# Fewer and larger load transfers in a one-token decoder block, with V6's products placed among head 7's scores

## The chip, the cores and the metric

The kernel runs on one core of a Trainium2 chip. The metric is device time in microseconds (us), the median of several executions. A profile is one execution of its own, with its own time. Its span runs from the first to the last instruction and is a little shorter than that time.

## What is computed

One token passes through a block with adaptive layer norm: attention over a cache, then a feed-forward layer with ReLU. Sizes: D = 512, 32 query heads on 8 heads of K and V ("head" below means one of these 8), 32,768 cached keys of 128 elements, Dff = 1792, all in bfloat16.

```python
mod = (silu(c) @ w_mod).reshape(6, 512)      # sa, ca, ga, sb, cb, gb
h = layernorm(x) * (1 + ca) + sa
q = h @ wq                                   # 32 heads of 128
p = softmax(q @ k.T / sqrt(128))             # 4 query heads for each K head
x = x + ga * ((p @ v) @ wo)
h = layernorm(x) * (1 + cb) + sb
out = x + gb * (relu(h @ w1) @ w2)
```

K and V are 8.4 MB a head each, 134 MB in all; the weights are another 15 MB.

## The kernel before

All loads are issued on SyncE's queue (SP) by `stream_dma` (L154), in the order of the list `stream` (L162 to L169). They go into a ring of three slots of 64 KB a partition (`ring`, L81). A slot holds one whole K or V of a head, or w_mod and wq together, or the "tail": wo, w1 and w2. The slots are used in turn, so V6 follows K6, V7 follows V5, and the tail follows K7. A load is issued when the last reader of its slot's old content is done, and loads are issued strictly in order. A load's key is (kind, head, steps): a head has four steps of 64 keys a partition (`NTILE`), and a load covers all four, two, or one of them. Before the change, K6, K7, V5 and V6 come in halves (`halves`, from `HALVED` = 5 on), the order at the end is K7 first half, V6 first half, K7 second half, V6 second half, and then V7 as a half and two quarters. wo comes in four pieces (`WOP`, L47: heads 0 to 3, 4 and 5, 6, 7), w2 in five (`W2P`). The second half of K0 is split unevenly over three transfers (`UNEVEN`, L57 and L137). After V0's issue SP runs `SPACE` drains (L146).

The order of TensorE (PE) and VectorE (DVE) is written out by hand from L637 on. For each head h:

- `turn_k` (L429) transposes K in place on VectorE, in blocks of 32 x 32. Heads before the last are turned a step at a time (128x4096 of f32), the last head half a step at a time (128x2048).
- `scores` (L450) makes 8 products for each half step on TensorE (L460). Steps 0 and 1 fill the first PSUM bank of the tile `S_ps`, steps 2 and 3 the second.
- For the last head, `bank_max` (L465) takes the maximum of each bank on its own. `softmax` (L468) is a generator; each `next(soft)` emits one more stage: the maximum, its transpose to a row (L478), the row's maximum, its way back (L492), the exponential on ScalarE (L497), the transpose of P (L502), the sum (L506), its reciprocal (L509).
- `pv` (L515) multiplies P with V: 16 products for each step (L523). Heads up to 4 run it as a loop on the chip, later heads as single instructions; `js` selects some of a step's 16 products.
- `blocks` (L548) scales and sums the result on VectorE, `o_cols` (L559) puts it into a column, and `normalise` (L568) prepares it for wo when the last head of a wo piece is done. `spread` (L582) and `project` (L593) multiply with wo: the first two pieces (`WOROWS`) as rows, 16 and 8 products of 512 columns, the last two as columns, 16 small products each (L605). `join_rows` (L614) transposes the rows on VectorE (L617) and adds them to the columns (L622).
- `keep_clock` (L630) makes products that nobody reads.

Heads 1 to 6 run through the loop at L647, where the scores of head g + 1 stand ahead of the products of head g with V. Head 7 is written out behind it (L675 to L735): the first half of K7 is turned and scored, then come `blocks` of head 5, the maximum of the first bank, and the 32 products of the first half of V6 (L691). Then the second half of K7 is turned and scored, half a step at a time, and the softmax of head 7 follows, with the rest of V6's products between its stages. Behind these stand V7's products, the projection with wo, the second layer norm, w1 (L765) and w2 (L788).

Of the kernel before, what the change touches and what calls it, by code (L numbers as in the profile page):

```python
# [10 lines left out]
F32 = mybir.dt.float32  # L11
# [6 lines left out]
def kernel(  # L18
# [14 lines left out]
    nc = tc.nc  # L33
# [10 lines left out]
    NTILE = Sk // (P * TK)  # L44
    NG = NTILE // 2

    WOP = [(0, Hkv // 2), (Hkv // 2, Hkv // 4), (Hkv - 2, 1), (Hkv - 1, 1)]  # L47
    WOROWS = 2
    LAST = Hkv - 1
    LOOPED = Hkv - 2  # L50
    HALVED = LOOPED - 1
    W2P = [(0, 5), (5, 10), (10, 12), (12, 13), (13, 14)]
    W1P = [(0, KT)]

    OUT0, OUT1 = 30, 34

    UNEVEN, EDGE, MOST = ("k", 0, (2, 3)), 2 * TK * Dh - D // 2, 111  # L57
    SPACE = 14
    assert Dh == 128 and REP == 4 and D == 512 and FT == W2P[-1][1] and NTILE == 4
    scale = float(Dh) ** -0.5  # L60
    eps = 1e-5
# [50 lines left out]
    def load(key):  # L112
        kind = key[0]
        if kind == "wm":
            t = piece("wmq_sb", 0, WM).rearrange("p (kt n) -> p kt n", kt=KT)
            src = wm_v
        elif kind == "wq":
            t = piece("wmq_sb", WM, WQ).rearrange("p (kt n) -> p kt n", kt=KT)
            src = wq_v
        elif kind in "kv":  # L120
            g, steps = key[1], key[2]
            src = (kv if kind == "k" else vv)[g, :, TK * steps[0]:TK * (steps[-1] + 1), :]
            name = f"Ksb{g}" if kind == "k" else f"Vsb{g}"
            t = piece(name, TK * Dh * steps[0], TK * Dh * len(steps)).rearrange("p (j d) -> p j d", d=Dh)
        elif kind == "wo":
            g0, n = WOP[key[1]]
            t = piece("tail_sb", g0 * REP * D, n * REP * D).rearrange("p (r d) -> p r d", d=D)
            src = wo_v(key[1])
        elif kind == "w1":
            k0, k1 = W1P[key[1]]  # L130
            t = piece("tail_sb", WO + k0 * Dff, (k1 - k0) * Dff).rearrange("p (kt f) -> p kt f", f=Dff)
            src = w1_v[:, k0:k1]
        else:
            f0, f1 = W2P[key[1]]
            t = piece("tail_sb", WO + KT * Dff + f0 * D, (f1 - f0) * D).rearrange("p (f d) -> p f d", d=D)
            src = w2_v[:, f0:f1]
        if key == UNEVEN:  # L137
            row, src_row = (x.rearrange("p j d -> p (j d)") for x in (t, src))
            for rows, cols in (
                (slice(0, P), slice(0, EDGE)), (slice(0, MOST), slice(EDGE, None)), (slice(MOST, P), slice(EDGE, None)),  # L140
            ):
                stream_dma(row[rows, cols], src_row[rows, cols])
        else:
            stream_dma(t, src)
        if key[:2] == ("v", 0):
            for _ in range(SPACE):  # L146
                nc.sync.drain()
        if kind in "kv":
            for i, u in enumerate(steps):
                loaded[(kind, g, u)] = t[:, TK * i:TK * (i + 1), :]  # L150
        else:
            loaded[key] = t

    def stream_dma(dst, src):  # L154
        i = nc.sync.dma_start(out=dst, in_=src)  # L155
        tc.stamp_issue_order_token(i.ins, "sp_stream")
        if last_loop:

            tc.add_manual_dep(i.ins, last_loop[0], mybir.DependencyInfo(
                mybir.DependencyClass.NoSync, mybir.DependencyReason.DATA))  # L160
# [1 line left out]
    whole, halves = [(0, 1, 2, 3)], [(0, 1), (2, 3)]  # L162
    stream = [("k", 0, halves[0]), ("wm",), ("wq",), ("k", 0, halves[1])]
    for g in range(LOOPED):
        stream += [("k", g + 1, s) for s in (halves if g >= HALVED else whole)] + [("v", g, s) for s in (halves if g >= HALVED else whole)]
    for s in halves:
        stream += [("k", LAST, s), ("v", LOOPED, s)]
    stream += [("v", LAST, (0, 1)), ("v", LAST, (2,)), ("v", LAST, (3,))] + [("wo", i) for i in range(len(WOP))]
    stream += [("w1", i) for i in range(len(W1P))] + [("w2", i) for i in range(len(W2P))]  # L169
    pos = [0]  # L170
# [72 lines left out]
    pick8 = const.tile([16, 8], BF16)  # L243
    nc.vector.tensor_tensor(out=pick8[:], in0=ident_bf[0:16, 0:8], in1=ident_bf[0:16, 8:16], op=ALU.add)
    cx_sel = const.tile([16, 2], BF16)
    nc.vector.tensor_copy(out=cx_sel[:], in_=cmask[8][0:16, 0:2])
    cx_bd = piece("wmq_sb", R0 + 2048 + 4 * P, D)[0:16].rearrange("p (b n) -> p b n", b=8)
    nc.vector.tensor_tensor(  # L248
        out=cx_bd, in0=cx_row[:].unsqueeze(1).to_broadcast([16, 8, D // 8]),
# [179 lines left out]
    def turn_k(g, u, half):  # L429

        if u == 0 and half == 0:
            S_tiles[g] = two_banks("S_ps")
            m_tiles[g] = spool.tile([P, NG], F32, tag="m2", name="m2") if g == LAST else None
        Ksb = need(("k", g, u))
        KTt = Ksb[:, 32 * half:32 * half + 32, :].rearrange("p j d -> p (j d)")
        KT_tiles[g, u, half] = KTt
        if g == 0 and u < 2 or g < LAST and half:
            return
        if g < LAST:
            KTt = Ksb.rearrange("p j d -> p (j d)")  # L440
        t = nc.vector.transpose(out=KTt.bitcast(F32), in_=KTt.bitcast(F32))  # L441
        behind_loop(t)
# [7 lines left out]
    def scores(g, u, half):  # L450

        t4 = (2 * u + half) % 4
        if t4 == 0:
            S_ps_tiles[g] = S_tiles[g][:, u // 2, :]
        KTv = KT_tiles.pop((g, u, half)).rearrange("p (jj h i par) -> p jj h i par", jj=32, h=2, i=32, par=2)
        for sl in range(2):
            s = 2 * t4 + sl
            for hp in range(4):
                h, par = hp // 2, hp % 2
                nc.tensor.matmul(  # L460
                    S_ps_tiles[g], lhsT=qbd[g % 2][:, hp, 4 * (7 - s):4 * (7 - s) + P], rhs=KTv[:, 16 * sl:16 * sl + 16, h, :, par],
                    start=(t4 == 0 and sl == 0 and hp == 0), stop=(t4 == 3 and sl == 1 and hp == 3),
                )
# [101 lines left out]
    def part_of(g):  # L565
        return [i for i, (g0, n) in enumerate(WOP) if g0 <= g < g0 + n][0]
# [26 lines left out]
    def project(i):  # L593

        n = WOP[i][1] * REP
        wo_sb = need(("wo", i))
        for r in range(n):
            if i < WOROWS:
                nc.tensor.matmul(
                    a_rows[0][32 * (r % 4):32 * (r % 4) + 1, :], lhsT=o2_tiles[i][:, r:r + 1],  # L600
                    rhs=wo_sb[:, r, :], start=False, stop=(i == WOROWS - 1 and r >= n - 4), skip_group_check=True,
                )
                continue
            for ko in range(KT):
                nc.tensor.matmul(  # L605
                    attnT_ps[:, ko:ko + 1],
                    lhsT=wo_sb[:, r, :].rearrange("p (m ko) -> p ko m", ko=KT)[:, ko, :],
                    rhs=o2_tiles[i][:, r:r + 1], start=False, stop=(i == len(WOP) - 1 and r == n - 1),
                    skip_group_check=True,
                )  # L610

    a_rows = []

    def join_rows():  # L614

        aT = room("tail_sb", TAIL, [P, 512])
        nc.vector.transpose(  # L617
            out=aT.rearrange("p (a ko m) -> p a ko m", a=4, ko=KT),
            in_=a_rows[0].rearrange("p (a m ko) -> p a ko m", a=4, ko=KT),
        )  # L620
        for a in range(4):
            nc.tensor.matmul(  # L622
                attnT_ps[32 * a:32 * a + 32, :], lhsT=place32[:],
                rhs=aT.rearrange("p (a ko m) -> p a ko m", a=4, ko=KT)[:, a, :, 0],
                start=False, stop=False, skip_group_check=True,
            )

    spare = []
# [8 lines left out]
    with tc.manual_schedule(engines={mybir.EngineType.PE, mybir.EngineType.DVE}):  # L637
# [36 lines left out]
            next(soft)  # L674
        g, h = LOOPED, LAST  # L675
        build_qbd(h)
        turn_k(h, 0, 0)
        turn_k(h, 0, 1)
        next(soft, None)
        turn_k(h, 1, 0)  # L680
        turn_k(h, 1, 1)
        blocks(g - 1)
        scores(h, 0, 0)
        scores(h, 0, 1)
        scores(h, 1, 0)
        o_cols(g - 1)
        scores(h, 1, 1)
        normalise(g - 1)
        spread(part_of(g - 1))
        bank_max(h, 0)  # L690
        pv(g, (0, 1))  # L691
        for u in (2, 3):
            for half in range(2):
                turn_k(h, u, half)
                scores(h, u, half)
        bank_max(h, 1)
        soft = softmax(h)
        next(soft)
        next(soft)
        next(soft)  # L700
        pv(g, (2,), range(6))
        next(soft)
        next(soft)
        open_o(LAST)
        pv(g, (2,), range(6, 16))
        pv(g, (3,))
        next(soft)
        next(soft, None)
        end_b.append(two_banks("end_ps"))
        a_rows.append(row_bank(end_b[0][:, 0, :]))  # L710
        blocks(g)
        pv(LAST, (0, 1))
        o_cols(LAST - 1)
        normalise(LAST - 1)
        pv(LAST, (2,))
        spread(2)
        hid_ps = ps_o.tile([P, 512], F32, tag="o", name="hid_ps")
        nc.vector.memset(hid_ps[:], 0.0)
        pv(LAST, (3,))
# [3 lines left out]
        project(0)  # L723
        keep_clock(2)
        o_cols(LAST)
        keep_clock(2)
        project(1)
        normalise(LAST)
        spread(3)
        keep_clock(2)  # L730
        project(2)
        keep_clock(1)
        join_rows()
        keep_clock(1)
        project(3)  # L735


        stat2 = const.tile([P, 2], F32)
# [88 lines left out]
```

## Time and profile before

| | |
|---|---|
| median of 3 runs | 354.37 us (354.16 to 354.63) |
| the profiled execution's own time | 354.42 us |
| its span | 352.6 us |
| TensorE busy | 272.3 us (77%) |
| VectorE busy | 195.6 us (55%) |
| ScalarE busy | 18.7 us (5%) |
| bytes read from HBM | 149.42 MB, 424 GB/s over the span |
| granted TensorE clock, mean | 0.926 |

How to read it: the page of the profile gives the busy time of each engine, the span in 40 slices (a digit is the busy share in tenths), the queues of the DMA engines, and the chain of work that ended last, followed back from the last instruction to what released each step. The timeline lists instructions in order of time: start, length, engine, source line, operation, output and inputs with shapes, count, and in square brackets the idle time of the engine ahead of it with what ended that. The view by windows gives each engine's busy time in stretches of the span, with the granted clock of TensorE. PE is TensorE's products, PEld its weight loads, DVE VectorE, ACT ScalarE, POOL GpSimd, SPq the queue of SyncE.

### The profile page before, as it was taken

What the parts mean: (1) busy time and instruction counts of PE and PEld (TensorE: products, weight loads), DVE (VectorE), ACT (ScalarE), POOL (GpSimd) and SP (SyncE); (2) the same over time, 40 slices, a digit from 0 to 9 for tenths busy, and PEclk for the clock granted to TensorE, in tenths of its full rate; (3) what the DMA queues carried; (4) which work ended last, traced back from release to release, by engine and by line L of the source; (5) the groups of instructions that cost most, each with busy time, mean ns of one, the idle gap of its engine ahead of it and who ended that gap; (6) DMA issues with size and microseconds to landing.
All of it is one profiled execution on the core that took longest, in us unless ns stands there. A gap on an engine that the chain in (4) does not pass through costs nothing. (4 is left out here: it accounts for less than half of the span.)

```text
span 352.6 us, 3544 instructions
## 1 busy us (share of the span) xinstructions
PE 272.3 (77%) x1310; PEld 111.8 (32%) x1310; DVE 195.6 (55%) x167; ACT 18.7 (5%) x37; POOL 6.0 (2%) x26
## 2 busy tenths in 40 slices
PE   0054980695999679884988499976999999789994
PEld 0021330232333224331333233322444443234442
DVE  7662563983079513965099316956674293743142
ACT  1200003001000010001000100001000100011000
POOL 3000000000000000000000000000000000000000
PEclk9996895698999969998999979996999999999999
DMA  8999989999999999999999999999999999999995
GB/s 353 404 432 456 468 387 461 446 401 446 439 424 440 416 439 446 401 455 446 409 453 446 409 453 431 426 394 439 446 414 427 450 429 424 431 453 398 432 426 213
DMA packets 5222, 149.57 MB, mean 424 GB/s; under 512 B 604, under 2 KB 988, under 8 KB 1628
## 3 DMA queue, kind: packets, MB, share of 16 engines
q1 hardware_dynamic: 5180, 149.43, 98.5%
q8 instruction: 8, 0.13, 0.1%
q14 instruction: 2, 0.02, 0.0%
q10 hardware_dynamic: 32, 0.00, 0.0%
HBM read 149.42 MB, written 0.00 MB: 424 GB/s over the span
## 5 line engine op out<-in xcount | busy, mean ns | idle before, releaser
L441 DVE STREAM_TRANSPOSE Ksb<-Ksb 128x4096 f32<-128x4096 f32 (+1 forms) x34 | 131.5, 3912 | 57.6 <-DMA Ksb<-in_A_k_cache_dram 57.6
L460 PE MATMUL S_ps<-Ksb,qbd 128*128 128x512 bf16 x512 | 118.9, 385 | 19.2 <-DVE Ksb L441 18.3
L523 PE MATMUL o_ps<-Vsb,P_g 128*16 (+1 forms) x512 | 124.3, 401 | 10.9 <-ACT P_g L497 10.0
L460 PEld LDWEIGHTS <-qbd 128*128 128x128 bf16 x512 | 49.2, 97 | 84.9 <-issue 27.6
L523 PEld LDWEIGHTS o_ps<-Vsb,P_g 128*16 x320 | 30.4, 95 | 60.0 <-issue 31.8
L523 PEld LDWEIGHTS <-P_g 128*16 128x16 bf16 x192 | 16.7, 90 | 22.9 <-issue 0.4
L473 DVE TENSOR_REDUCE m_p<-S_ps 128x1 f32<-128x1024 f32 x7 | 8.6, 1223 | 21.8 <-PE S_ps L460 21.8
L502 DVE STREAM_TRANSPOSE P_g<-P_g 128x1024 bf16<-128x1024 bf16 x8 | 10.0, 1245 | 15.6 <-ACT P_g L497 15.6
L494 ACT ACTIVATE nbias<-Mb_ps 128x1 f32<-128x1 f32 x8 | 1.4, 171 | 269.5 <-PE Mb_ps L492 269.5
L324 PE MATMUL mod_ps<-wmq_sb,siluT 128*1 128x512 bf16 x24 | 3.6, 624 | 9.9 <-DMA wmq_sb<-in_w_mod_dram 9.9
L332 DVE STREAM_TRANSPOSE Ksb<-Ksb 128x4096 f32<-128x4096 f32 x2 | 8.8, 4424 | 1.7 <-DMA Ksb<-in_A_k_cache_dram 1.7
L478 PE MATMUL mT_ps<-ident_f,m_p 128*1 128x128 f32 x8 | 2.2, 270 | 8.9 <-DVE m_p L473 7.9
L497 ACT ACTIVATE P_g<-S_ps,nbias 128x1024 bf16<-128x1024 f32 x8 | 8.9, 1114 | 0.2
L560 PE MATMUL acc_ps<-mask_sb,Y 16*128 16x4 f32 x16 | 3.4, 282 | 5.1 <-DVE Y L556 5.1
L552 DVE SCALAR_TENSOR_TENSOR o_ps<-o_ps,Linv,smask 16x512 f32<-16x512 f32 x8 | 5.8, 720 | 2.8 <-PE o_ps L523 2.8
L254 PE MATMUL xc_ps<-cx_sel,wmq_sb 16*128 16x2 bf16 x4 | 0.3, 172 | 8.7 <-DVE wmq_sb L248 8.7
L590 DVE CAST o_sb<-o_ps 128x4 bf16<-128x4 f32 (+2 forms) x4 | 0.7, 167 | 11.1 <-PE o_ps L586 11.1
L415 POOL TENSOR_TENSOR qbd<-qrep_sb,rowpick 128x64 bf16<-128x64 bf16 x8 | 2.4, 299 | 228.0 <-PE S_ps L460 198.3
L509 DVE RECIPROCAL Linv<-L_ps 16x1 f32<-16x1 f32 x8 | 1.0, 126 | 8.3 <-PE L_ps L506 8.3
L556 DVE TENSOR_REDUCE Y<-o_ps 16x128 f32<-16x512 f32 x8 | 5.4, 679 | 0.3
L635 PE MATMUL spare_ps<-qbd,ident_bf 128*128 128x512 bf16 x18 | 5.4, 381 | 0.0
L396 PE MATMUL q_ps<-wmq_sb,hT 128*1 128x512 bf16 x32 | 3.6, 626 | 2.3 <-DMA wmq_sb<-in_A_wq_dram 2.3
(114 smaller groups left out, 71.6 us busy)
## 6 DMA issues: line engine op xcount, KB each, us to landing
Ksb<-in_A_k_cache_dram SPq DMA_DIRECT2D x5, 4096.0 KB, 22.9
Vsb<-in_A_v_cache_dram SPq DMA_DIRECT2D x5, 4096.0 KB, 36.5
wmq_sb<-in_A_wq_dram SPq DMA_DIRECT2D x1, 4096.0 KB, 28.1
Vsb<-in_A_v_cache_dram SPq DMA_DIRECT2D x2, 2048.0 KB, 41.1
Ksb<-in_A_k_cache_dram SPq DMA_DIRECT2D x1, 4032.0 KB, 37.2
wmq_sb<-in_w_mod_dram SPq DMA_DIRECT2D x1, 3072.0 KB, 18.9
tail_sb<-in_A_wo_dram SPq DMA_DIRECT2D x1, 2048.0 KB, 23.2
tail_sb<-in_B_w_dram SPq DMA_DIRECT2D x1, 1792.0 KB, 30.6
```

The lines of the kernel that those rows point to most:

```text
L324: nc.tensor.matmul(dst[j // 4][32 * (j % 4):32 * (j % 4) + 1, :], lhsT=src_T[:, kt:kt + 1], rhs=w[:, kt, j * 512:(j + 1) * 512], start=(kt ...
L332: nc.vector.transpose(out=t, in_=t)
L396: nc.tensor.matmul(q_ps[i][32 * a:32 * a + 1, :].rearrange("o (h e) -> o h e", e=32), lhsT=hT[:, kt:kt + 1], rhs=wq_f[:, kt, i, a], start= ...
L441: t = nc.vector.transpose(out=KTt.bitcast(F32), in_=KTt.bitcast(F32))
L460: nc.tensor.matmul(S_ps_tiles[g], lhsT=qbd[g % 2][:, hp, 4 * (7 - s):4 * (7 - s) + P], rhs=KTv[:, 16 * sl:16 * sl + 16, h, :, par], start= ...
L473: behind_loop(nc.vector.reduce_max(out=m_p[:], in_=S_g.rearrange("p g f -> p (g f)"), axis=AX.X))
L497: nc.scalar.activation(out=P_g[:], in_=S_g.rearrange("p g f -> p (g f)"), func=ACT.Exp, bias=nbias[:], scale=scale, accum_out=l_g[:],)
L502: behind_loop(nc.vector.transpose(out=P_g[:], in_=P_g[:]))
L523: nc.tensor.matmul(o_tiles[g][:], lhsT=PT, rhs=Vx, start=first, stop=False, skip_group_check=True)
L552: nc.vector.scalar_tensor_tensor(out=o, in0=o, scalar=Linv_tiles.pop(g)[:], in1=smask[:].unsqueeze(2).to_broadcast([16, 4, Dh]), op0=ALU.m ...
L556: nc.vector.tensor_reduce(out=Y[:], in_=o.rearrange("p s d -> p d s"), op=ALU.add, axis=AX.X)
L635: nc.tensor.matmul(spare[0], lhsT=ident_bf[:], rhs=qbd[0][:, :, 0:P], start=True, stop=True)
```

## The change

The list of loads has 29 entries in place of 37 transfers. K0's second half is one transfer again. K6, K7 and V5 come whole. The order at the end is K7, the two halves of V6, V7 as before, wo in two pieces (heads 0 to 3 and 4 to 7), w1, and w2 in four pieces. SP runs 19 drains in place of 14 after V0's issue.

In the part of head 7, `blocks` of head 5 comes first, then all eight half steps of K7 are turned, then all are scored. Behind each of the last four groups of scores stand three products of V6's step 0. `bank_max` of the first bank stands, on VectorE, behind the eight turns. The rest of V6's products follow in and behind the softmax of head 7: 4 of step 0, step 1, then steps 2 and 3 together.

At the end, both pieces of wo are used as rows with 16 products each, the second one only after head 7's result has been spread. The products as columns go. Six spare products stand ahead of the second piece and three behind it. The constant `cx_sel`, until now cut out of a mask for wo pieces of 8 rows, gets a small reduce of its own.

```diff
-    WOP = [(0, Hkv // 2), (Hkv // 2, Hkv // 4), (Hkv - 2, 1), (Hkv - 1, 1)]
-    WOROWS = 2
+    WOP = [(0, Hkv // 2), (Hkv // 2, Hkv // 2)]
-    W2P = [(0, 5), (5, 10), (10, 12), (12, 13), (13, 14)]
+    W2P = [(0, 6), (6, 11), (11, 13), (13, 14)]
-    UNEVEN, EDGE, MOST = ("k", 0, (2, 3)), 2 * TK * Dh - D // 2, 111
-    SPACE = 14
+    SPACE = 19
...
-        if key == UNEVEN:
-            row, src_row = (x.rearrange("p j d -> p (j d)") for x in (t, src))
-            for rows, cols in (
-                (slice(0, P), slice(0, EDGE)), (slice(0, MOST), slice(EDGE, None)), (slice(MOST, P), slice(EDGE, None)),
-            ):
-                stream_dma(row[rows, cols], src_row[rows, cols])
-        else:
-            stream_dma(t, src)
+        stream_dma(t, src)
...
     for g in range(LOOPED):
-        stream += [("k", g + 1, s) for s in (halves if g >= HALVED else whole)] + [("v", g, s) for s in (halves if g >= HALVED else whole)]
-    for s in halves:
-        stream += [("k", LAST, s), ("v", LOOPED, s)]
+        stream += [("k", g + 1, whole[0]), ("v", g, whole[0])]
+    stream += [("k", LAST, whole[0])] + [("v", LOOPED, s) for s in halves]
...
-    nc.vector.tensor_copy(out=cx_sel[:], in_=cmask[8][0:16, 0:2])
+    cx_half = const.tile([16, 2], F32)
+    nc.vector.tensor_reduce(
+        out=cx_half[:], in_=ident_f[0:16, 0:16].rearrange("p (c r) -> p c r", r=8), op=ALU.add, axis=AX.X,
+    )
+    nc.vector.tensor_copy(out=cx_sel[:], in_=cx_half[:])
...
         for r in range(n):
-            if i < WOROWS:
-                nc.tensor.matmul(
-                    a_rows[0][32 * (r % 4):32 * (r % 4) + 1, :], lhsT=o2_tiles[i][:, r:r + 1],
-                    rhs=wo_sb[:, r, :], start=False, stop=(i == WOROWS - 1 and r >= n - 4), skip_group_check=True,
-                )
-                continue
-            for ko in range(KT):
-                nc.tensor.matmul(
-                    attnT_ps[:, ko:ko + 1],
-                    lhsT=wo_sb[:, r, :].rearrange("p (m ko) -> p ko m", ko=KT)[:, ko, :],
-                    rhs=o2_tiles[i][:, r:r + 1], start=False, stop=(i == len(WOP) - 1 and r == n - 1),
-                    skip_group_check=True,
-                )
+            nc.tensor.matmul(
+                a_rows[0][32 * (r % 4):32 * (r % 4) + 1, :], lhsT=o2_tiles[i][:, r:r + 1],
+                rhs=wo_sb[:, r, :], start=False, stop=(i == len(WOP) - 1 and r >= n - 4), skip_group_check=True,
+            )
...
         build_qbd(h)
-        turn_k(h, 0, 0)
-        turn_k(h, 0, 1)
         next(soft, None)
-        turn_k(h, 1, 0)
-        turn_k(h, 1, 1)
         blocks(g - 1)
-        scores(h, 0, 0)
-        scores(h, 0, 1)
-        scores(h, 1, 0)
-        o_cols(g - 1)
-        scores(h, 1, 1)
-        normalise(g - 1)
-        spread(part_of(g - 1))
-        bank_max(h, 0)
-        pv(g, (0, 1))
-        for u in (2, 3):
+        for u in range(NTILE):
             for half in range(2):
                 turn_k(h, u, half)
+        for u in range(NTILE):
+            for half in range(2):
                 scores(h, u, half)
-        bank_max(h, 1)
+                if u >= 2:
+                    first = 3 * (2 * u + half - 4)
+                    pv(g, (0,), range(first, first + 3))
+                elif half:
+                    (o_cols if u == 0 else normalise)(g - 1)
+            if u % 2:
+                bank_max(h, u // 2)
         soft = softmax(h)
         next(soft)
         next(soft)
         next(soft)
-        pv(g, (2,), range(6))
+        pv(g, (0,), range(12, 16))
         next(soft)
         next(soft)
         open_o(LAST)
-        pv(g, (2,), range(6, 16))
-        pv(g, (3,))
+        pv(g, (1,))
         next(soft)
         next(soft, None)
         end_b.append(two_banks("end_ps"))
         a_rows.append(row_bank(end_b[0][:, 0, :]))
+        pv(g, (2, 3))
         blocks(g)
...
         pv(LAST, (2,))
-        spread(2)
...
         project(0)
         keep_clock(2)
         o_cols(LAST)
+        normalise(LAST)
         keep_clock(2)
+        spread(1)
+        keep_clock(6)
         project(1)
-        normalise(LAST)
-        spread(3)
-        keep_clock(2)
-        project(2)
-        keep_clock(1)
+        keep_clock(3)
         join_rows()
-        keep_clock(1)
-        project(3)
```

More of the change, by code (lines that the diff above doesn't have):

```diff
@@ L624, in join_rows @@
                 rhs=aT.rearrange("p (a ko m) -> p a ko m", a=4, ko=KT)[:, a, :, 0],
-                start=False, stop=False, skip_group_check=True,
+                start=False, stop=True, skip_group_check=True,
             )
```

## The prediction

> **What bounds the kernel now.** I read the page first: span, the load queue's share, the chain that ended last.
>
> ```profile
> span 352.6 us, 3544 instructions
> DMA  8999989999999999999999999999999999999995
> q1 hardware_dynamic: 5180, 149.43, 98.5%
> DMA 19%; PE 5%; DVE 3%; SPq 0%; issue 0%
> ```
>
> The queue of loads is busy for 98.5% of the span, and the chain is mostly DMA. The stream of loads sets the time; TensorE and VectorE have only to keep up and to free the three ring slots. Next, the same chain in order of time, for the last 80 us (start, length, what).
>
> ```profile
> 272.40 29.53 DMA Ksb<-in_A_k_cache_dram
> 301.96 8.90 DVE Ksb L441 x4
> 310.90 1.91 PE S_ps L460 x8
> 313.20 25.28 DMA tail_sb<-in_A_wo_dram
> 338.50 11.12 DMA tail_sb<-in_B_w_dram
> 349.66 0.29 PE end_ps L788 x4
> ```
>
> The second half of K7 lands at 301.93; four turns of it and its scores follow; they free the slot, and wo is issued into it at 313.2. The chain steps over to the queue there, but the queue isn't empty: wo lands 25 us later because V7 stands before it. The last w2 piece lands at 349.62, and 3.0 us of arithmetic end the span. What matters is how far the engines are behind those landings. The timeline of TensorE:
>
> ```profile
> 271.93 7.07 PE L523 MATMUL o_ps<-Vsb,P_g 128*16 128x512 bf16 x32
> 286.88 0.19 PE L506 MATMUL L_ps<-l_g,mask_sb 128*16 128x1 f32 x2
> 295.26 7.07 PE L523 MATMUL o_ps<-Vsb,P_g 128*16 128x512 bf16 x32
> 310.90 1.90 PE L460 MATMUL S_ps<-Ksb,qbd 128*128 128x512 bf16 x8 [0.30 <-DVE Ksb L441]
> 313.77 0.27 PE L478 MATMUL mT_ps<-ident_f,m_p 128*1 128x128 f32 x1 [0.97 <-DVE m_p L475]
> 313.98 1.46 PE L523 MATMUL o_ps<-Vsb,P_g 128*16 128x512 bf16 x6
> 315.52 5.78 PE L523 MATMUL o_ps<-Vsb,P_g 128*16 128x512 bf16 x26
> 321.39 7.07 PE L523 MATMUL o_ps<-Vsb,P_g 128*16 128x512 bf16 x32
> 332.36 3.62 PE L523 MATMUL o_ps<-Vsb,P_g 128*16 128x512 bf16 x16
> 336.08 1.03 PE L599 MATMUL end_ps<-tail_sb,o_sb 128*1 128x512 bf16 x16
> ```
>
> The first half of V6's products (295.26, 32 of them) is done while TensorE would else wait for K7's second half. After the last scores (312.80), 6 + 26 products of V6 and 64 of V7 remain, and V7's last ends at 335.98. Call that moment E. Behind it:
>
> ```profile
> 338.52 0.60 PE L599 MATMUL end_ps<-tail_sb,o_sb 128*1 128x512 bf16 x8
> 341.01 0.67 PE L605 MATMUL acc_ps<-o_sb,tail_sb 128*128 128x1 bf16 x16
> 341.71 0.16 DVE L740 TENSOR_TENSOR x1T<-acc_ps,modT_sb 128x4 f32<-128x4 f32 x1 [1.65 <-PE acc_ps L605]
> 345.33 0.93 PE L765 MATMUL hid_ps<-tail_sb,h2T 128*1 128x448 bf16 x16 [1.28 <-DMA tail_sb<-in_B_w_dram]
> 347.10 0.73 PE L788 MATMUL end_ps<-tail_sb 128*32 128x128 bf16 x20
> 349.98 0.28 DVE L793 TENSOR_TENSOR o_rows<-end_ps,gb_rows 34x128 f32<-34x128 f32 x1 [2.95 <-PE end_ps L788]
> ```
>
> W1's products wait 1.28 us for their load, so between E and the end the engines have about 2 us to spare, no more. A change that makes E later by over 2 us makes the kernel later.
>
> **The change, part by part.**
>
> *Fewer transfers.* Eight fewer. 1.5% of the span, 5.3 us, is all that the queue is not busy, its start and end included: 0.14 us for each of 37 transfers at the very most, 1.1 us for eight; at the least nothing. K0's second half loses its uneven split, at most 64 KB (0.15 us at 4,096 KB in 9.7 us, below) that move to other engines. I take nothing for the stream as a whole, being nearer to a queue without gaps, and keep -1.1 to +0.2 us for K7's landing.
>
> The Trainium skill's page "DMA: Bandwidth & Descriptors", section "Anatomy of one DMA", puts a fixed 2.0 us on each DMA (measured there for DMAs issued from GpSimd); eight fewer would by that estimate save 16 us. The 5.3 us that the queue lacks in all do not bear that out for transfers queued one behind another.
>
> *K7 ahead of all of V6.* At 272.40 three transfers of 4,096 KB stand in the queue (K7's first half, V6's first, K7's second) and take 29.53 us: about 9.7 us each after the rest of V5. Whole K7 therefore lands one transfer earlier than its second half did: 301.93 - 9.7 = 292.2. K6 lands whole five transfers before 301.93, at 253.5. Is VectorE free for K7?
>
> ```profile
> 258.09 8.74 DVE L441 STREAM_TRANSPOSE Ksb<-Ksb 128x4096 f32<-128x4096 f32 x2
> 232.38 3.64 PE L460 MATMUL S_ps<-Ksb,qbd 128*128 128x512 bf16 x16 [0.69 <-DVE Ksb L441]
> 292.36 0.68 DVE L556 TENSOR_REDUCE Y<-o_ps 16x128 f32<-16x512 f32 x1
> 295.45 0.68 DVE L466 TENSOR_REDUCE m<-S_ps 128x1 f32<-128x512 f32 x1
> ```
>
> K6's four turns (two in 8.74) end at 253.5 + 17.6 = 271.1, its last 16 scores at 274.8, against 272.0 before. V5's 64 products and the sums of head 6 follow as they do now (271.93 to 287.07, 15.1): 290.0. blocks(5), a product and a sum of about 0.7 each, ends at 291.5, before K7 is there. V6, K7's successor in the queue, is issued at 275 and V7 at 290, both with over 15 us of loads queued. The delay of 3 us is hidden by K7's own 19.4 us of transfer.
>
> *K7's turns and scores.* Here the change pays. VectorE now gets all eight turns in a row, then bank_max(7,0), the maximum over the first PSUM bank. Eight at 2.22 (8.90 for four): 292.2 + 17.8 = 310.0. TensorE does the scores of steps 0 and 1 behind the first four turns, until about 303. Then it should go on with step 2, turned at 303.3. In the program as built it can't: the first product of step 2 waits for a count of VectorE that only bank_max(7,0) brings (the turns of steps 2 and 3 no longer raise the count one by one), since it opens the second bank of the same tile that bank_max reads. Before, bank_max stood ahead of those turns (295.45), and the wait cost nothing. Now it stands behind all eight: 310.0 + 0.7 = 310.7. Queued behind the waiting product on TensorE is everything else: 3 products of V6 after each score group, the softmax, V6, V7, wo. So TensorE idles some 7.5 us with V6's first half landed (301.9) and unused.
>
> From 310.7, at 0.22 a product (7.07 for 32): 32 scores and the 9 products of V6 among them, 41 x 0.22 + 0.14 = 9.2: last score 319.9 (now 312.80). The maximum's way to the next transpose takes 0.97 as now: 320.9. Then 0.2, 4 products 0.9 and Mb: 322.05. V6's second step, 16 x 0.22 = 3.5, the sum 0.2, steps 2 and 3, 7.05: 332.8. V7's products with the column product between them now take 321.39 to 335.98, 14.6, of which 0.1 is a spread that goes: 14.5. E = 347.3, so far without a clock loss.
>
> *The clock.* The same idle time is in the trace once, where head 1's turns are waited for:
>
> ```profile
> 64.77 12.29 PE L460 MATMUL S_ps<-Ksb,qbd 128*128 128x512 bf16 x48 [7.41 <-DVE Ksb L441]
> 64.77:68.09 3.32, 3.32 (x8) 1.15 (x8) 0.50 1.09 474
> 68.09:77.06 8.97, 8.97 (x41) 3.82 (x40) 1.00 0.94 409
> ```
>
> After 7.41 us of idling the granted clock is 0.50 for 3.32 us; 48 products take 12.29 where 48 x 0.22 + 0.14 = 10.7 would do: 1.6 lost. The length of such a stretch varies with where it begins, so I keep 1.0 to 2.8 and take the nearest row: E = 348.9.
>
> *wo, and the tail.* Both pieces are now rows, so what follows E on TensorE is in series:
>
> ```profile
> 337.05 0.60 PE L635 MATMUL spare_ps<-qbd,ident_bf 128*128 128x512 bf16 x2
> 337.59 0.38 PE L560 MATMUL acc_ps<-mask_sb,Y 16*128 16x4 f32 x2
> 339.35 0.71 DVE L617 STREAM_TRANSPOSE tail_sb<-end_ps 128x512 f32<-128x512 f32 x1
> ```
>
> project(0) 1.0, two spare products 0.5, the column product 0.3 (its input, blocks(7), takes 1.5 beside these), two spares 0.5, the spread, six spares 1.3, project(1) 1.0, the transpose 0.8 with three spares beside it, four joining products 0.3: x1T starts 5.9 after E (5.7 now, with waits for wo's pieces, which land by 341.0 and are no longer late). From x1T to W1's products 2.4 (3.6 now, less the wait of 1.28), from these to w2's first 1.8 as now, 56 products at 0.036 and their drain 2.2, o_rows to the end of the span 352.6 - 350.0 = 2.7. Together 15.0, less 0.1 for overlaps of those rounded up: 14.9.
>
> w2's pieces and wo land as now, 10 us before they are used; wo's issue moves from 313 to 321, and V7, queued until about 331, covers that. If scores ended after 331, the queue would run dry and each us more would be one more. The small reduce for cx_sel and five more drains stand where the stream is far ahead; 0.2 us if that cover were gone.
>
> **Sum.** 292.2 + 17.8 + 0.7 + 9.2 + 1.0 + 1.15 + 10.75 + 14.5 = 347.3; + 1.6 + 14.9 = 363.8. The span was 352.6, so +11.2. The profiled execution took 354.42, 1.8 more than its span, and the runs' median was 354.37: the two agree. Forecast **365.6 us**.
>
> **The rivals.**
> 1. *The products of step 2 don't wait for bank_max.* If a turn alone releases them, they start at 303.4, and 8 scores with 3 products of V6 (2.4 to 2.6) keep pace with a turn (2.22) with little lag: last score at 313.0, E at 340.5 instead of 347.3, end at 355.4, time 357.2, or up to 358.7 if the 4 us of idling before K7's first scores brings a half clock. Taken: 357.9. For it: the two banks are different bytes. Against it: the built program's wait. 0.08.
> 2. *The half clock lasts longer or comes twice.* Two stretches in place of one, another 1.6 to 3: about 368.5. For it: the idling of 4 us at 290 to 294 and of 7.5 at 303. Against it: the first is absorbed, since TensorE is early for bank_max anyhow. 0.06.
> 3. *The stream still sets the end* (the other side). That needs E by about 338, that is TensorE done with V6's first half before K7's last scores, as now. Then the end is 3.0 behind the last landing, moved by -1.1 to +0.2: 353.3 to 354.6. By the skill's fixed cost it would be 338; the queue's 98.5% is against that. Against all of it: 96 products of V6 and V7 alone are 21 us, and with 23 more of V6 left behind the last score than now, E is 5 us later even with no wait at all. 0.02 for a gain of about 1.1, 0.01 for no change.
>
> **How the numbers follow.** The forecast has 0.83, the rivals 0.08, 0.06 and 0.03. Its own bounds: landing of K7 -1.1 to +0.2, clock -0.6 to +1.2, the tail's series 0.7 either way; not all at one end: 363.4 to 367.8. With rival 2's nearer part the range is 363.3 to 368.3, which leaves out some 2 in 10: rivals 1 and 3 and the tails. 0.2%, 0.7 us, is about what a measurement of this kernel can tell from no change. Faster 0.02, same 0.01, slower 0.97.
>
> **What would show it.** In the profile after: eight turns in a row from about 292.2, the reduce of bank_max at 310.0, TensorE idle about 7.5 us ahead of step 2's scores, released by that reduce; granted clock 0.5 from 310.7 for some 3 us; wo issued near 321; W1's products without a wait for DMA; the chain of waits at the end on TensorE and VectorE, back to K7's landing. Wrong if scores of step 2 begin near 303.4 (rival 1), if the last w2 piece still ends the span (rival 3), or if K7 lands elsewhere than 291 to 293, which moves all by as much.

## The result, and the profile after

| | before | after |
|---|---|---|
| median, 6 runs each, same chip | 354.19 us (354.10 to 354.63) | 365.69 us (365.17 to 366.29) |
| ratio, 95% interval | | 1.0323 (1.0309 to 1.0336) |
| the profiled execution: time, span | 354.42, 352.6 | 365.17, 363.4 |
| load transfers | 37 | 29 |

The changed kernel is 11.5 us slower; 365.6 was forecast. Two of the six executions of run 10 below fell into a slower state (366.5 and 369.5 us) and are left out of its figures. The page of the changed kernel: span, DMA slices, load queue, and the chain that ended last, by engine.

```profile
span 363.4 us, 3488 instructions
DMA  8999999999999999999999998999899999999930
q1 hardware_dynamic: 4184, 149.42, 95.4%
PE 13%; DMA 9%; DVE 6%; issue 0%; ACT 0%; ACTq 0%
```

The same megabytes now leave the queue idle at the end: the last two slices are 3 and 0, where before the last was 5 and all others 8 or 9. TensorE leads the chain in place of DMA. The same chain in order of time (start, length, what):

```profile
257.77 34.48 DMA Ksb<-in_A_k_cache_dram
...
292.28 17.66 DVE Ksb L435 x8
309.94 0.59 DVE m L460
...
310.57 3.54 PE S_ps L454 x8
...
327.82 13.84 PE o_ps L517 x64
...
358.95 1.76 PE end_ps L764 x54
```

No transfer stands in it after K7's landing at 292.25. K7's eight turns, then the maximum over the first bank (L460), then TensorE's products for nearly all the rest; behind V7's last product TensorE and VectorE take turns. TensorE's timeline (start, length, operation, count, idle time ahead of it):

```profile
294.64 6.40 PE L454 MATMUL S_ps<-Ksb,qbd 128*128 128x512 bf16 x16 [4.72 <-DVE Ksb L435]
...
301.28 3.65 PE L454 MATMUL S_ps<-Ksb,qbd 128*128 128x512 bf16 x16
310.57 3.54 PE L454 MATMUL S_ps<-Ksb,qbd 128*128 128x512 bf16 x8 [5.64 <-DVE m L460]
...
314.79 1.91 PE L454 MATMUL S_ps<-Ksb,qbd 128*128 128x512 bf16 x8
...
319.97 1.91 PE L454 MATMUL S_ps<-Ksb,qbd 128*128 128x512 bf16 x8
...
348.59 0.38 PE L517 MATMUL o_ps<-Vsb,P_g 128*16 128x512 bf16 x1
...
357.18 0.93 PE L741 MATMUL hid_ps<-tail_sb,h2T 128*1 128x448 bf16 x16
```

Step 2's first eight scores (310.57) stand behind 5.64 us of idling that the maximum ended, and take 3.54 where each later group takes 1.91. V7's last product ends at 348.59 + 0.38 = 348.97, the moment E of the prediction, 13 us later than before (335.98). W1's products (357.18) wait for no load. The granted clock of the same stretch, by windows (the first number behind the brackets is PEclk):

```profile
293.50:300.30 6.80, 5.66 (x14) 1.98 (x14) 6.80 (x4) 0.00 (x0) 0.00 (x0) 0.50 1.04 446
300.30:307.10 6.80, 4.62 (x22) 1.94 (x20) 6.80 (x4) 0.00 (x0) 0.00 (x0) 1.00 0.93 400
307.20:313.90 6.70, 3.33 (x8) 0.97 (x7) 3.31 (x3) 0.00 (x0) 0.00 (x0) 0.50 1.03 445
```

Two stretches at half clock, 6.8 us each. The first makes steps 0 and 1 slow, which costs nothing, since TensorE then waits anyhow; of the second, half lies in the idle time, and 3.3 us meet work.

### The profile page after: what moved, and what is told of

Read it like the earlier page. It is cut to its first block, busy times and chain, and to the rows that moved or that the text cites. A ratio compares the mean times of both kernels' runs of the same rounds, so it can differ in the third digit from the quotient of the medians.

```text
span 363.4 us, 3488 instructions
## 1 busy us (share of the span) xinstructions
PE 277.2 (76%) x1289; PEld 111.8 (31%) x1289; DVE 194.1 (53%) x160; ACT 18.7 (5%) x37; POOL 5.6 (2%) x24
## 5 line engine op out<-in xcount | busy, mean ns | idle before, releaser
L454 PE MATMUL S_ps<-Ksb,qbd 128*128 128x512 bf16 x512 | 124.5, 397 | 28.4 <-DVE Ksb L435 21.8
L517 PE MATMUL o_ps<-Vsb,P_g 128*16 (+1 forms) x512 | 124.6, 402 | 10.8 <-ACT P_g L491 10.0
L454 PEld LDWEIGHTS <-qbd 128*128 128x128 bf16 x512 | 50.3, 99 | 98.2 <-issue 44.5
L460 DVE TENSOR_REDUCE m<-S_ps 128x1 f32<-128x512 f32 x2 | 1.3, 671 | 11.4 <-PE S_ps L454 11.4
L620 PE MATMUL spare_ps<-qbd,ident_bf 128*128 128x512 bf16 x23 | 6.2, 381 | 0.0
L475 DVE TENSOR_REDUCE Mrow<-mT_ps 1x4 f32<-1x128 f32 x8 | 2.2, 274 | 5.6 <-PE mT_ps L472 5.6
```

Source lines behind the costliest of these rows:

```text
L454: nc.tensor.matmul(S_ps_tiles[g], lhsT=qbd[g % 2][:, hp, 4 * (7 - s):4 * (7 - s) + P], rhs=KTv[:, 16 * sl:16 * sl + 16, h, :, par], start= ...
L517: nc.tensor.matmul(o_tiles[g][:], lhsT=PT, rhs=Vx, start=first, stop=False, skip_group_check=True)
L620: nc.tensor.matmul(spare[0], lhsT=ident_bf[:], rhs=qbd[0][:, :, 0:P], start=True, stop=True)
```

## The experiments

The theory was: the reduce of `bank_max(7, 0)`, put behind all eight turns, holds step 2's scores, and with them everything that TensorE has queued; the half clock adds a little; fewer transfers give and cost nothing. Rivals: TensorE would be as late without the wait; the new order of the loads, or the larger transfers, are the cost.

| kernel | median, us | ratio to before, 95% interval |
|---|---|---|
| changed, one maximum over both banks | 356.86 (4 runs) | 1.0073 (1.0055 to 1.0091) |
| changed, maximum two turns earlier | 359.11 (4) | 1.0137 (1.0119 to 1.0156) |
| changed, spare products in the gap | 363.46 (4) | 1.0258 (1.0240 to 1.0277) |
| changed, 32 products of V6 in the gap | 357.11 (4) | 1.0095 (1.0071 to 1.0118) |
| before, maximum late | 358.98 (4) | 1.0139 (1.0121 to 1.0157) |
| before, 32 transfers | 354.80 (11) | 1.0014 (1.0005 to 1.0023) |
| before, wo in two pieces as rows | 354.75 (11) | 1.0014 (1.0005 to 1.0023) |
| changed, head 7 as before, 30 transfers | 354.44 (11) | 1.0008 (0.9999 to 1.0017) |
| the same with 29 transfers | 354.65 (11) | 1.0015 (1.0006 to 1.0024) |
| before, both halves of K7 ahead of V6 | 356.56 (4) | 1.0067 (1.0053 to 1.0082) |
| the same with spare products | 354.72 (11) | 1.0014 (1.0005 to 1.0023) |

The kernel before took 354.14 to 354.27 beside them (medians).

**1. Take the wait away: one maximum over both banks.** The two calls of `bank_max` go, and head 7's softmax reduces the whole tile at once, as the other heads do.

```diff
-            m_tiles[g] = spool.tile([P, NG], F32, tag="m2", name="m2") if g == LAST else None
+            m_tiles[g] = spool.tile([P, NG], F32, tag="m2", name="m2") if False else None
...
-        if g < LAST:
+        if m2 is None:
...
-            if u % 2:
-                bank_max(h, u // 2)
```

> The changed kernel with one maximum over both banks of head 7's scores, behind the last score, in place of the two bank_max; nothing else. The first product of step 2 then waits for its own turn alone. Theory (the wait for the first bank's maximum, behind eight turns, costs most of the 11.5 us): step 2's scores start near 304.9 in place of 310.6, at full clock, the last score ends near 314.5 in place of 321.9; the longer maximum (1.22 in place of 0.69 + 0.16) gives 0.4 back; 7.0 us faster than the changed kernel, 358.7 us. Rival (the order of V6's products, 55 of them behind the last score in place of 32, is the cost, the wait is hidden): within 1 us of 365.7. Rival (only the half clock behind the idling costs): 364.0.

Measured 356.86, 8.8 us less than the changed kernel, where 7.0 were expected. Its profiled execution was the slowest of the four (357.9; the others 356.66 to 356.88). TensorE's timeline of it:

```profile
301.13 5.38 PE L454 MATMUL S_ps<-Ksb,qbd 128*128 128x512 bf16 x24
306.44 0.81 PE L517 MATMUL o_ps<-Vsb,P_g 128*16 128x512 bf16 x3
...
341.32 0.38 PE L517 MATMUL o_ps<-Vsb,P_g 128*16 128x512 bf16 x1
```

Step 2's first scores follow those of step 1 with no gap (24 in 5.38), and E is 341.70. So between the medians the late maximum costs 8.8 of the 11.5 us, and about 2.7 are left that it doesn't explain. Between the two profiled executions it is 7.3 of 10.8 (spans 363.4, 356.1 and 352.6; E moves by 7.27). A likely reason for the gap: this kernel has no wait that hides the first stretch at half clock, 6.8 us long in its profile, and with one of 3.4 us, as in runs 2 and 4, step 2's scores would start 1.1 sooner. Its other three executions were 1.0 to 1.2 us faster, but have no trace.

**2. Move the wait: the maximum after the sixth turn.**

```diff
-        for u in range(NTILE):
+        for u in range(3):
             for half in range(2):
                 turn_k(h, u, half)
...
+        bank_max(h, 0)
+        for half in range(2):
+            turn_k(h, 3, half)
```

> The changed kernel with the maximum of the first bank moved on VectorE from behind the eighth turn to behind the sixth; the wait stays, its place alone changes. Theory: the maximum waits for step 1's scores (304.9), ends near 305.7, step 2's scores start there, the two turns behind it are early enough, last score near 315.3; 6.6 us faster than the changed kernel, 359.1 us. Rival (V6's order is the cost): within 1 us of 365.7.

Measured 359.11. On its TensorE:

```profile
306.19 1.90 PE L454 MATMUL S_ps<-Ksb,qbd 128*128 128x512 bf16 x8 [2.34 <-DVE m L460]
```

The scores start 4.38 us sooner than in the changed kernel (310.57), still released by the reduce, and the first eight take 1.90 and not 3.54: two turns (4.4) and 1.6 of clock make 6.0, which is what separates the two profiled spans (363.4 and 357.4); the medians are 6.6 apart. The end follows the place of this one reduce.

**3. Keep the wait, keep the clock.** 24 spare products, which nobody reads, ahead of step 2's scores.

```diff
+                if u == 2 and not half:
+                    keep_clock(24)
                 scores(h, u, half)
```

> The changed kernel with 24 spare products on TensorE (5.3 us at 0.22, read by nobody) ahead of step 2's scores, so that it is busy while it would wait; the wait itself stays. Theory: the granted clock stays at full through 310.6 to 314, the 8 scores there take 1.8 in place of 3.5 us, and the end comes 1.7 us earlier: 364.0 us. If the half clock has another cause than idling: 365.7. If the spare products delay step 2's scores: above 365.7.

Measured 363.46, 2.2 us less than the changed kernel:

```profile
304.78 5.34 PE L620 MATMUL spare_ps<-qbd,ident_bf 128*128 128x512 bf16 x24
310.56 1.90 PE L454 MATMUL S_ps<-Ksb,qbd 128*128 128x512 bf16 x8 [0.44 <-DVE m L460]
```

The scores start at the same time and take 1.90 in place of 3.54: 1.64 shown in one execution, 2.2 between the medians. In the profiled executions the 5.64 us of idling and 1.64 of clock add up to the 7.3 of run 1; between the medians 6.6 of the 8.8 are left for the waiting.

**4. Fill the wait: V6's 32 early products in the gap**, none among the scores. The reduce stays late.

```diff
+            if u == 2:
+                pv(g, (0, 1))
...
-                if u >= 2:
-                    first = 3 * (2 * u + half - 4)
-                    pv(g, (0,), range(first, first + 3))
-                elif half:
+                if u < 2 and half:
```

(The rest of V6's products stand as before the change.)

> The changed kernel with all 32 products of V6's steps 0 and 1 ahead of step 2's scores, where TensorE waits for the maximum, and none among the scores; the wait stays. Theory (idle time is the price, and work that doesn't depend on the maximum can fill it): products 304.9 to 312.0, scores at full clock from 312.0, last score 319.2 in place of 321.9, and 32 products of V6 behind it in place of 55, another 5.1 us: 7.8 us faster than the changed kernel, 357.9 us. Rival (the wait is hidden and the scores' own pace counts): the last score later by up to 7 us, no gain.

Measured 357.11 (357.9 was expected):

```profile
303.66 7.07 PE L517 MATMUL o_ps<-Vsb,P_g 128*16 128x512 bf16 x32
310.67 7.12 PE L454 MATMUL S_ps<-Ksb,qbd 128*128 128x512 bf16 x32
...
340.18 0.38 PE L517 MATMUL o_ps<-Vsb,P_g 128*16 128x512 bf16 x1
```

The scores start as late as in the changed kernel, and yet 8.6 us are back: the wait costs what stands behind it, and needed work put ahead of it is as good as no wait. E is 340.56.

**5. Make the wait alone, in the kernel before.** K7's second half is turned first, then comes the maximum, then the scores.

```diff
-        bank_max(h, 0)
         pv(g, (0, 1))
         for u in (2, 3):
             for half in range(2):
                 turn_k(h, u, half)
+        bank_max(h, 0)
+        for u in (2, 3):
+            for half in range(2):
                 scores(h, u, half)
```

> The kernel before with one part of the change: the turns of K7's second half all ahead of the first bank's maximum, and that ahead of the scores of steps 2 and 3. Loads and all else as before. Theory: four turns end at 310.9, the maximum at 311.5, step 2's scores start there in place of 304.3, TensorE having idled 9 us since V6's first half, so the half clock adds 1.7; last score near 320.4 in place of 312.8, and of these 7.6 us some 2.5 are covered by waits for loads at the end: 5.1 us slower than before, 359.3 us. Rival (the wait is hidden): 354.2.

Measured 358.98, 4.8 us over before:

```profile
311.46 8.55 PE L460 MATMUL S_ps<-Ksb,qbd 128*128 128x512 bf16 x32 [8.89 <-DVE m L466]
...
342.60 0.38 PE L523 MATMUL o_ps<-Vsb,P_g 128*16 128x512 bf16 x1
```

8.89 us of idling ended by the reduce, and 8.55 us for 32 scores that take 7.12 in the run above; E is 342.98. One wait without any other part of the change makes the kernel slower.

**6 and 7. Fewer transfers alone, and wo alone, in the kernel before.** The first joins K0's second half, K6 and V5 and takes w2 in four (32 transfers). The second takes wo in two pieces as rows, with the changed kernel's series behind E (35 transfers).

```diff
-    W2P = [(0, 5), (5, 10), (10, 12), (12, 13), (13, 14)]
+    W2P = [(0, 6), (6, 11), (11, 13), (13, 14)]
...
-        stream += [("k", g + 1, s) for s in (halves if g >= HALVED else whole)] + [("v", g, s) for s in (halves if g >= HALVED else whole)]
+        stream += [("k", g + 1, whole[0]), ("v", g, whole[0])]
```

```diff
-    WOP = [(0, Hkv // 2), (Hkv // 2, Hkv // 4), (Hkv - 2, 1), (Hkv - 1, 1)]
+    WOP = [(0, Hkv // 2), (Hkv // 2, Hkv // 2)]
...
-        project(2)
-        keep_clock(1)
+        keep_clock(6)
+        project(1)
+        keep_clock(3)
         join_rows()
```

> The kernel before with K0's second half, K6 and V5 whole and w2 in four pieces, 32 load transfers for 37; the order of K7 and V6 in halves and the four pieces of wo stay. Theory (transfers queued one behind another cost next to nothing): K6's scores and V5's products 3 us later, covered ahead of K7's second half; 354.2 us, 0.3 either way. Rival (each transfer costs the queue up to 0.14 us): 353.5 us. Rival (a fixed 2.0 us each): 344 us.

> The kernel before with wo in two pieces, both used as rows, and the changed kernel's series of steps behind V7's products; the loads of K and V, and head 7, stay. Theory: the second piece lands whole at 341.0, its 16 products, the transpose and the join put x1T at 343.2 in place of 341.7, 1.5 later, w1's products start 0.3 later, and w2's last piece still sets the end: 354.2 to 354.6 us. Rival (the series of steps is a cost of its own): 1.2 later, 355.4 us.

Measured 354.80 and 354.75: no gain, which rules out both rivals of run 6. They are 0.7 and 0.6 over before and 0.3 and 0.15 above the upper ends of their forecasts; that is within the 0.2% that the prediction takes for no change, though the intervals leave out 1. VectorE's last sum, first of the 32 transfers, then of wo in two pieces (before: 349.98):

```profile
349.97 0.28 DVE L786 TENSOR_TENSOR o_rows<-end_ps,gb_rows 34x128 f32<-34x128 f32 x1 [2.92 <-PE end_ps L781]
```

```profile
349.74 0.28 DVE L792 TENSOR_TENSOR o_rows<-end_ps,gb_rows 34x128 f32<-34x128 f32 x1 [2.80 <-PE end_ps L787]
```

Five transfers fewer bring the end of the arithmetic 0.01 us forward. What is lost (0.4 us of span, 353.0 for 352.6, and 0.6 between the medians) is lost behind it.

**8 and 9. The changed kernel with head 7 as before**: K7 and V6 in alternating halves, V6's 32 products and the maximum ahead of K7's second half; all else stays as changed. The second takes w2 in three pieces, so that it has 29 transfers too.

```diff
-    stream += [("k", LAST, whole[0])] + [("v", LOOPED, s) for s in halves]
+    for s in halves:
+        stream += [("k", LAST, s), ("v", LOOPED, s)]
...
+        bank_max(h, 0)
+        pv(g, (0, 1))
+        for u in (2, 3):
             for half in range(2):
                 turn_k(h, u, half)
-        for u in range(NTILE):
-            for half in range(2):
                 scores(h, u, half)
```

> The changed kernel with head 7's part as before it: K7 and V6 loaded in alternating halves, V6's 32 early products ahead of K7's second half, the maximum of step 1's bank ahead of the second half's turns; kept are K0 unsplit, K6 and V5 whole, wo in two pieces used by rows and w2 in four (30 transfers). Theory (the order of K7 and V6 and what head 7 does with it is the whole cost, the fewer transfers cost and gain nothing in the stream): x1T near 343.0, the hidden layer's products near 345.25, the last piece of w2 lands near 349.3 and sets the end, 354.1 to 354.5, of which up to 0.3 by the place of out's landing among the last waits. Rival 1 (whole K6 and V5, or wo in two pieces, cost something that the changed kernel's longer path covered): 355.0 or more. Rival 2 (fewer transfers gain): 353.5 or less.

> As the run before it, with w2 in three pieces (9, 4 and 1 of its 14 chunks; 29 transfers), by which out's landing is the last of the final waits again, as in the kernel before and the changed one. Theory: 354.0 to 354.3, the last landing of w2 near 349.3 sets the end. Rival 1 (larger transfers cost): 355.0 or more. Rival 2 (fewer transfers gain): 353.5 or less.

Measured 354.44 and 354.65: 11.2 and 11.0 us less than the changed kernel. Head 7's part, its loads with it, carries nearly the whole cost; neither version beats the kernel before. The second is 0.35 above its forecast range. VectorE's last sum in the first of the two, and what its SP waited for (waited by whom, for what: us, times, longest):

```profile
349.50 0.28 DVE L774 TENSOR_TENSOR o_rows<-end_ps,gb_rows 34x128 f32<-34x128 f32 x1 [2.78 <-PE end_ps L769]
```

```profile
SPq L803 <- DMA out_dram<-o_bf: 0.7, 1, 0.7
```

The arithmetic ends 0.48 us sooner than before (349.98), but the span by only 0.1 (352.5), and SP's last waits now list 0.7 us for out's landing, a wait that this view doesn't have for the kernel before. I took the place of that wait among the last ones for the reason. The version with 29 transfers was made so that it comes last again, and it was no faster. That explanation fell. The changed kernel and runs 1 to 4 list the wait too (0.5), and yet end 2.6 to 2.7 us after their last sum starts, as the kernel before does. Why runs 6 to 9 lose 0.2 to 0.7 us of their profiled spans behind the arithmetic stays open.

**10 and 11. The order of the loads alone, in the kernel before**, and the same with 26 spare products, which nobody reads, ahead of V6's first products.

```diff
-    for s in halves:
-        stream += [("k", LAST, s), ("v", LOOPED, s)]
+    for key in (("k", LAST), ("v", LOOPED)):
+        stream += [key + (s,) for s in halves]
```

```diff
         bank_max(h, 0)
+        keep_clock(26)
         pv(g, (0, 1))
```

> The kernel before with the order of four loads alone changed: both halves of K7, then both halves of V6. Head 7's part is as before, so V6's 32 early products stand ahead of K7's last scores and wait for V6's first half, now at 301.9. Theory (the order costs by what it keeps TensorE waiting for): TensorE idles from 295.3 to 301.9, 6.6 us; products of V6 to 309.0, the 32 scores, turned long before, in one go to 316.1, V7's last product 3.3 us later than before at 339.3, and by the late kernel's tail of 13.9 us the span 353.2 without a clock loss; with a half clock after the idling 1.0 to 2.8 more. Time 356.6 (356.0 to 357.8). Rival 1: the order is free, 354.2. Rival 2: it makes up the whole remainder of the runs without the late maximum even with a warm clock, and more with a cold one: 358 or more.

> As the run before it, with 26 spare products, which nobody reads, ahead of V6's first products, to keep the clock up over the idling (295.3 to 301.0). Theory: V6's products 301.9 to 309.0, scores to 316.1, V7's last product 339.3, span 353.2, time 355.0 (354.8 to 355.5): the order alone costs 0.8, and the rest of what is left without the late maximum comes from turning K7 only when it is whole and from V6 products left behind the last score. Rival 1: the order is free, 354.2. Rival 2: the order is the whole remainder, 356.9 to 357.1.

Measured 356.56 and 354.72 (the second 0.1 under its forecast range). TensorE in the first, then in the second:

```profile
302.14 8.73 PE L523 MATMUL o_ps<-Vsb,P_g 128*16 128x512 bf16 x32 [5.78 <-DMA Vsb<-in_A_v_cache_dram]
...
340.52 0.38 PE L523 MATMUL o_ps<-Vsb,P_g 128*16 128x512 bf16 x1
```

```profile
301.98 7.07 PE L523 MATMUL o_ps<-Vsb,P_g 128*16 128x512 bf16 x32 [0.36 <-DMA Vsb<-in_A_v_cache_dram]
...
338.70 0.38 PE L523 MATMUL o_ps<-Vsb,P_g 128*16 128x512 bf16 x1
```

V6's half lands 6 us after TensorE is ready for it. With a warm clock E is 339.08, 3.1 us later than before, and only 0.6 of that reaches the time. The idle time itself was nearly free; the half clock behind it made E 1.8 later still and cost 1.8.

**What the 11.5 us are made of.** 8.8 the late maximum, of it 2.2 clock (1, 3). 0.6 the order of the loads (11). From E to the end of the span the changed kernel's series takes 14.4 (363.4 - 348.97; 356.1 - 341.70 in 1, 355.0 - 340.56 in 4), the kernel before's, where E is late, 13.9 (356.9 - 342.98 in 5, 354.8 - 340.90 in 10): 0.5 for wo in two pieces. It lies ahead of x1T, the first sum behind the projection, which starts 5.91 after E in the former and 5.35 in the latter, and it counts only where E is late: in run 7 x1T starts 1.2 later than before (342.95), and W1's products, which wait for their load before the change, no later (345.25). That leaves some 1.6 that no run has alone: K7 turned only when it is whole, so that TensorE comes to V6 at 303.66 in 4 and at 301.98 in 11. This last reading is argued from two timelines, not shown by a kernel of its own. The small parts are good to 1 us at best: the profiled spans leave 3.5 and not 2.7 for them together, and the 0.6 of run 11 is about what runs 6, 7 and 9 lose without that order (0.5 to 0.7).

## Why the prediction was right

- **K7's landing.** Forecast 292.2, measured 292.25. Counting transfers of one size back from a known landing was good to 0.1 us, and taking no gain for fewer transfers was right: 0.01 us in run 6.
- **The turns and the maximum.** VectorE of the changed kernel:

```profile
292.28 17.66 DVE L435 STREAM_TRANSPOSE Ksb<-Ksb 128x2048 f32<-128x2048 f32 x8 [0.77 <-DMA Ksb<-in_A_k_cache_dram]
309.86 0.65 DVE L460 TENSOR_REDUCE m<-S_ps 128x1 f32<-128x512 f32 x1
...
354.88 0.16 DVE L716 TENSOR_TENSOR x1T<-acc_ps,modT_sb 128x4 f32<-128x4 f32 x1 [0.37 <-PE acc_ps L607]
```

  Forecast 310.0 and 310.7; they end at 309.9 and 310.5. This step decides everything, and it came from the waits of the program as built, not from the diff: the diff shows a maximum over one bank beside scores into another. Runs 1 and 2 show that the wait is real. That it is there because the two banks are one tile is read from the built program; no run gives each bank a tile of its own.
- **The idle time and the clock.** Forecast 7.5 us idle, measured 5.64: steps 0 and 1 ran at half clock from 293.5 on, so TensorE came 2 us later to the same wait. The prediction named that and counted it as absorbed, which it was. Rival 2 had two stretches, and there were two; it was wrong about their price. For the second, 1.6 was forecast; eight scores took 3.54 in place of 1.90, and run 3 gives 2.2 between the medians. The stretch is 6.8 us long, not some 3 from the wait's end on: the first half of it passed while TensorE idled. In the row that the 1.6 came from, the same had been overlooked: head 1's half clock lasts from 54.4 to 68.1 in the kernel before, and the 3.32 us are only what was left of it when the wait ended. That 3.3 us met work both times, and so the size came out, is luck.
- **E.** Forecast 348.9, measured 348.97. The last scores start at 319.97 and end at 321.9, 0.4 later than the forecast with the clock's 1.6 in it; V6 and V7 gave 0.3 back. The chain is right, but the agreement to 0.1 us comes from errors that cancel.
- **The tail.** The sum that starts x1T (last row above) is at 354.88, E + 5.9 as forecast. W2's 56 products were counted at 2.2 with their drain, from 0.036 each. Measured:

```profile
358.95 1.74 PE L764 MATMUL end_ps<-tail_sb 128*32 128x128 bf16 x56
```

  0.4 less, because they now come in one go with no load to wait for. That is the difference between the span forecast, 363.8, and the 363.4 measured. The profiled execution was the fastest of six; the median was 365.69, so 0.5 us between executions hides this error in the forecast of the time.
- **The rivals.** Rival 1 gave 357.2 to 358.7 without the wait; run 1, which takes it away, took 356.86, 0.3 under its low end. Rival 3, that the stream still sets the end, failed at the first row of the chain.

Where the working was rough: it charged all of the 11.2 us to one chain and never said what would be left without the wait, beyond rival 1's time. Some 2.7 us are left, which the runs put down to three smaller causes, the largest of them argued only.

## What to carry to other kernels

When a queue of loads is busy nearly without gaps (98.5% of the span here), don't expect a gain from fewer transfers: five fewer gave nothing (run 6). What counts is how late the engines are behind each landing. Look up what an instruction waits for in the built program: here a reduce over one half of a tile held back the writes into the other half, which the source doesn't show. Where a wait can't be taken away, put work that is needed anyway ahead of it (run 4: 8.6 us), which also keeps the clock up.

## What the runs showed of the hardware

- The stretches at half clock have lengths near multiples of 3.4 us in these traces: 6.8 twice in the changed kernel (293.5 to 300.3 and 307.1 to 313.9), 3.4 in runs 2 (295.2 to 298.6) and 4 (294.6 to 298.0), 13.7 in the kernel before at head 1 (54.4 to 68.1). Windows just inside two of them, of run 2 and of the kernel before:

```profile
295.25:298.60 3.35, 3.35 (x9) 1.16 (x8) 3.35 (x2) 0.00 (x0) 0.00 (x0) 0.50 0.86 372
```

```profile
54.45:68.05 13.60, 3.49 (x10) 1.38 (x11) 9.05 (x4) 2.62 (x4) 0.00 (x0) 0.50 0.99 429
```

  Of the second, TensorE is busy for 3.49 us only: most of a stretch can pass unseen in idle time. With the short stretch, steps 0 and 1 lose less: 16 scores took 5.32 and 5.31 us in runs 2 and 4, against 6.40. The changed kernel's times spread over 1.1 us, those of the kernel with spare products in the gap over 0.3; stretches of differing length or place would fit that, but four to six runs don't show it.
- The end of this kernel isn't fixed. From the start of the same last sum to the end of the span there were 2.6 us before (352.6 - 349.98), 3.4 in run 7 (353.1 - 349.74) and 3.0 in run 8 (352.5 - 349.50), with the same program behind it. A gain of half a us ahead of that point was lost there.
